# A recurrent attention with a gated projection: the list scheduler's order replaced by one written order

## Chip, cores and metric

The kernel runs on one core of one Trainium2 chip, in one launch. The metric is the device time of the launch in microseconds (us), median of several runs.

## The reference, cut to what matters

```
# r, k, v, w, a, b: (B=4, H=8, S=768, D=40); moe_w_a, moe_w_b: (320, 1536); moe_w_out: (1536, 320)
state = zeros(B, H, D, D)
for t in range(S):
    y[t]  = r[t] @ state                         # per batch and head
    Sa    = state @ a[t]
    state = state * w[t] - outer(Sa, b[t]) + outer(v[t], k[t])
x = y as (B*S, H*D)                              # 3072 x 320
out = ((x @ moe_w_a) * (x @ moe_w_b)) @ moe_w_out
```

The first half is a recurrence over 768 tokens for 32 pairs of batch and head. The second half is a gated projection of the 3072 rows that it gives.

## The kernel before

The 768 tokens are cut into 12 chunks of 64 (n = 0 to 11), and each chunk's 32 heads into two halves (c = 0, 1). Inside a chunk the recurrence is written as matrix products with the inverse of a triangular 64x64 matrix per head. The work is planned as 3159 operations, each a short run of instructions of one engine. They come from these functions inside `wkv_moe`:

- `prep(n, c)` loads a half chunk (`W`, `BK`, `A`), runs two scans and a reciprocal over it on VectorE (`Q<-W`, `d`, `pe<-W`), multiplies (`BK<-BK,Q`, `A<-A,pe`), computes 64 small products on TensorE (`scores`: `at<-A,BK`) and transposes (`nat`: `at<-ident,BK`), masks a part on VectorE (`TK<-at,tri`), copies the other on ScalarE (`AB<-at`) and stores all of it by DMA to `un_d`, from where `un` is loaded later.
- `lanes(g)` inverts the triangular matrices of a group of one or two chunks on VectorE, 15 or 31 steps of two instructions (`Yt<-Y,N` and `Y<-Y,Yt`), between one transposition at its start (`N<-AB`) and two at its end (`TC<-Y` and `T<-Y`). `T` is the list's name for the tile `T3`.
- `join(n)` and `merge(n)` put the inverses together on TensorE (operations `xt`, `t3`, `tc_`, `l2a`, `l2b`; tiles `T,AB`, `W,TC`, `TC,W`).
- `main(n, c)` is the recurrence itself: on TensorE `r_`, `u_`, `s_`, `g_`, `y_` and `sd_`, between them copies on ScalarE and products on VectorE. The state of a half is in `ST`; it is updated by a sum and a product (`ST<-at,ST`, `ST<-ST,pcs`), and `sd_` transposes it (`at<-ident,ST`). The output goes to `X` and by DMA to `x_d`.
- `pack(n)` loads a chunk's rows back and splits them into two parts of lower precision (`xk`).
- `plan_tile(f)` and `plan_lazy(f)` load one of 12 tiles of the three weights (`wraw`) and decode it, in some 13 operations each piece on VectorE, ScalarE and GpSimd (`w_ex`, `w_mt`, `w_rs`, then `wt` or `wo`).
- `unit(n, f)` is one chunk's rows times one tile of the weights: 16 matmuls into `ab`, the product of the two halves (`g`), its split into `gh` and `gl`, and six matmuls into `po` (operation `second`). There are 144 units. Five of the tiles are used while the recurrence runs, the seven others after it, for all chunks.

What sets the order: `Plan.op` notes each operation with its engine, an estimate of its duration, what it reads and writes, and a rank `v`. `Plan.run` (line 158 on) is a list scheduler. It keeps a clock for each engine, takes the engine that can start first, and on it, among the operations that can start within 0.05 us of the first, the one with the lowest rank. It also hands out the four PSUM banks `at` (`Banks`, `need`, `free`). The chosen operation is emitted at once, and every engine runs its instructions in the order of emission; SP issues all DMAs in that order too. So a waiting instruction holds everything behind it on its engine. `InOrder` keeps the framework from moving anything.

All instructions that pass through `InOrder` carry its line, 72 in the profile before (203 after). So the rows below are told apart by their tiles.

## Time and profile before

| what | us |
|---|---|
| median of 3 runs (their range) | 796.56 (795.31 to 804.69) |
| span of the profiled execution, first to last instruction | 799.3 |
| TensorE (PE) busy in it | 705.0 |
| VectorE (DVE) busy in it | 573.6 |
| ScalarE (ACT) busy in it | 417.0 |
| mean granted TensorE clock, share of 2.4 GHz | 0.889 |

The profiled execution lies 2.7 us above the median and within the range of the runs. What lies around its span is not told apart from it, so a sum made in its trace is carried to the median by that difference. A busy time is a sum over stages with different limits, and a stretch is therefore read by its own row.

### The profile page before, as it was taken

To read this page: it belongs to the slowest core of one execution; us is meant where nothing else is said; L and a number is where in the kernel's file an instruction comes from. 1 tells how busy PE (TensorE), PEld (TensorE's weight loads), DVE (VectorE), ACT (ScalarE), POOL (GpSimd) and SP (SyncE) were. 2 spreads that over 40 slices of the span, in tenths; PEclk is the share of its full clock that TensorE was granted. 3 is DMA by queue.
4 is the path that set the end of the run, shared out by engine and by line. 5 is a ranking of instruction groups with operands and counts; after the bars stand their busy time and mean duration, and the time that the engine had idled before them with its cause. 6 is when DMAs were issued, how large, how long until landed. Compare 5 with 4: busy or idle time off the path is not lost.

```text
span 799.3 us, 31281 instructions
## 1 busy us (share of the span) xinstructions
PE 705.0 (88%) x13509; PEld 665.0 (83%) x13509; DVE 573.6 (72%) x1161; ACT 417.0 (52%) x1080; POOL 195.9 (25%) x242
## 2 busy tenths in 40 slices
PE   5446757889789999899899999999999999999996
PEld 3346646878679998789888898999999999999996
DVE  8779798678978998898898684675676574233244
ACT  4438637636666577458555454855764443222221
POOL 6000203200120121102011010364546563222221
PEclk9555655789769999999999698999999999999999
DMA  6879886496878688977857367747621210000023
GB/s 195 245 212 275 257 246 196 114 276 205 234 231 262 194 221 242 292 248 199 260 161 210 88 219 214 212 118 195 197 75 54 58 42 5 1 1 2 1 78 125
DMA packets 99915, 133.05 MB, mean 166 GB/s; under 512 B 28554, under 2 KB 76026, under 8 KB 96954
## 3 DMA queue, kind: packets, MB, share of 16 engines
q1 hardware_dynamic: 99770, 130.97, 54.9%
q8 instruction: 108, 1.77, 0.9%
q14 instruction: 37, 0.30, 0.1%
HBM read 87.86 MB, written 38.43 MB: 158 GB/s over the span
## 4 chain that ended last, share of the span: by engine, by line
PE 75%; DMA 10%; issue 4%; DVE 4%; ACT 3%; SPq 2%; POOL 1%; ACTq 0%; DVEq 0%; POOLq 0%
PE ab L72 34%; PE at L72 26%; PE po L72 15%; DMA BK<-in_bk_dram 2%; DMA un_d<-bkn 2%; SPq L72 2%; DMA un<-un_d 1%; DMA wraw<-in_wa_dram 1%; DMA acc<-po_d 1%; DMA un_d<-TK 1%; DMA xf<-x_d 1%; DMA W<-in_wd_dram 1%; DMA SV<-in_vn_dram 1%; ACT T L72 1%; DMA A<-in_ai_dram 1%
## 5 line engine op out<-in xcount | busy, mean ns | idle before, releaser
L72 PE MATMUL ab<-xk,wt 120*128 120x256 f32 x2304 | 310.7, 289 | 2.0 <-issue 1.5
L72 PEld LDWEIGHTS ab<-xk,wt 120*128 120x128 f32 x2304 | 294.2, 195 | 5.1 <-issue 1.8
L72 POOL TENSOR_TENSOR gl<-g,gh 128x256 fp32r<-128x256 f32 x134 | 108.8, 813 | 367.2 <-ACT gh L72 338.7
L72 PE MATMUL po<-wo,gh 128*128 128x320 f32 x576 | 151.2, 316 | 3.7 <-ACT w_rs L72 2.8
L72 DVE TENSOR_TENSOR g<-ab,g 128x256 f32<-128x256 f32 x144 | 60.7, 422 | 112.4 <-ACT g L72 111.9
L72 ACT COPY g<-ab 128x256 f32<-128x256 f32 x144 | 53.7, 373 | 125.2 <-PE ab L72 120.7
L72 PEld LDWEIGHTS po<-wo,gh 128*128 128x128 f32 x576 | 102.1, 189 | 2.6 <-ACT gh L72 0.8
L72 ACT CAST gh<-g 128x256 fp32r<-128x256 f32 x144 | 58.4, 406 | 71.9 <-PE po L72 36.3
L72 PE MATMUL po<-wo,gl 128*128 128x320 f32 x288 | 89.2, 310 | 0.0
L72 DVE TENSOR_TENSOR Y<-Y,Yt 128x31 f32<-128x31 f32 (+20 forms) x185 | 64.2, 347 | 6.4
L72 PE MATMUL at<-SV,un 128*64 128x40 f32 (+1 forms) x1472 | 53.3, 238 | 16.8 <-DMA SV<-in_vn_dram 11.0
L72 PEld LDWEIGHTS at<-SV,un 128*64 128x64 f32 (+1 forms) x1472 | 47.7, 149 | 22.7 <-issue 16.5
L72 DVE TENSOR_TENSOR Yt<-Y,N 128x31 f32<-128x31 f32 (+20 forms) x185 | 63.6, 344 | 3.9
L72 DVE TENSOR_TENSOR acc<-po,acc 128x320 f32<-128x320 f32 x96 | 43.8, 487 | 24.7 <-PE po L72 24.7
L72 PEld LDWEIGHTS po<-wo,gl 128*128 128x128 f32 x288 | 54.8, 190 | 2.9 <-DVE Y L72 2.9
L72 PE MATMUL at<-A,BK 64*64 64x64 f32 x1536 | 36.4, 256 | 17.6 <-DVE A L72 10.3
L72 PEld LDWEIGHTS at<-A,BK 64*64 64x64 f32 x1536 | 32.4, 166 | 21.6 <-issue 12.4
L72 POOL TENSOR_TENSOR w_mt<-w_mt,wt 120x384 f32<-120x384 f32 x22 | 23.8, 1083 | 87.6 <-ACT wt L72 74.4
L72 ACT COPY AB<-at 32x256 f32<-32x256 f32 (+1 forms) x72 | 31.5, 437 | 22.4 <-PE at L72 19.5
L72 ACT COPY SV<-at 64x160 f32<-64x160 f32 x96 | 27.4, 286 | 21.9 <-PE at L72 20.6
L72 DVE TENSOR_TENSOR G<-at,tri 128x512 f32<-128x512 f32 x48 | 30.9, 683 | 11.2 <-PE at L72 10.8
L72 PE MATMUL at<-T,AB 32*32 32x32 f32 x1152 | 23.2, 213 | 16.9 <-DVE T L72 7.7
(108 smaller groups left out, 1155.2 us busy)
## 6 DMA issues: line engine op xcount, KB each, us to landing
un<-un_d SPq DMA_DIRECT2D x22, 1092.0 KB
BK<-in_bk_dram SPq DMA_DIRECT2D x22, 448.0 KB
rv<-in_rvf_dram SPq DMA_DIRECT2D x22, 448.0 KB
un_d<-bkn SPq DMA_DIRECT2D x22, 320.0 KB
x_d<-X SPq DMA_DIRECT2D x24, 256.0 KB
un_d<-pe SPq DMA_DIRECT2D x22, 260.0 KB
un_d<-A SPq DMA_DIRECT2D x44, 128.0 KB
un_d<-TK SPq DMA_DIRECT2D x44, 128.0 KB
```

What stands on the lines that cost most here:

```text
L72: r = fn(*args, **kwargs)
```

## The change

`Plan.run` no longer chooses. It takes a list of the 3159 operations' numbers and emits them in that order. The clock of each engine is still kept, because the banks are still chosen by it. The branch for filler work, which was not in use, and two switches that were always on are gone. Two dependencies that held before because of the old order are stated: the second copy into `SV` (operation `uc`) reads what the first wrote, and the second product into `X` reads what the first wrote. Both pairs run on one engine each, ScalarE and VectorE. No operation is added or removed, and each has the same instructions as before; the tiles `at` that it gets may differ.

```
+ORDER = """
+0 3 4 8 5 2 7 1 6 15 19 21 24 22 27 25 26 16 17 18 23 28 243 20 43 246 247 266 9 11 13 244 12 32 248 33 29 40 62 34 38
...
+"""
...
-    def run(self, slack=0.05, switch=0.13):
+    def run(self, order, switch=0.13):
...
-        while todo:
...
-                s0 = min(s for s, _ in c)
-                s, o = min(((s, o) for s, o in c if s <= s0 + slack), key=lambda x: (x[1].v, x[1].seq))
...
+        assert sorted(order) == list(range(len(self.ops)))
...
+        for k in order:
+            o = self.ops[k]
+            assert o.left == 0
+            s = max(engines[o.eng], o.ready)
...
-            pl.op("ACT", 2 * act(160), uc, [("u", q)], [(*kS, j)] if j == 0 else [kS])
+            pl.op("ACT", 2 * act(160), uc, [("u", q), (*kS, 0)] if j else [("u", q)], [kS] if j else [(*kS, 0)])
...
-                in1=PEt[:, gq * 4:gq * 4 + 4, 0:C]), [("y", q), kU], [(*kX, gq)] if gq == 0 else [kX], free=[(ps, gq)], v=v + 0.15)
+                in1=PEt[:, gq * 4:gq * 4 + 4, 0:C]), [("y", q), kU, (*kX, 0)] if gq else [("y", q), kU], [kX] if gq else [(*kX, 0)], free=[(ps, gq)], v=v + 0.15)
...
-    pl.run()
+    pl.run([int(k) for k in ORDER.split()])
```

Where the order changes, at three places. First VectorE, at the beginning of the first inverse (`lanes` of chunk 0; `BK_182`, `A_184` are chunk 1's first half, `BK_183` its second). Before:

```order
L72 TENSOR_TENSOR BK_182<-BK_182,Q_180 128x1024
L72 STREAM_TRANSPOSE N<-AB 128x32x32
L72 TENSOR_TENSOR A_184<-A_184,pe_188 128x512
L72 TENSOR_TENSOR BK_183<-BK_183,Q_181 128x1024
L72 TENSOR_TENSOR AB<-AB,off 128x16x32
L72 SCALAR_TENSOR_TENSOR Q_180<-W_178,one 128x521
L72 TENSOR_TENSOR TK_186<-at_65,tri 128x512
L72 RECIPROCAL d_190<-Q_180 128x8
L72 SCALAR_TENSOR_TENSOR pe_188<-W_178,d_190 128x520
L72 TENSOR_TENSOR Yt<-Y,N 128x30
```

The same place now:

```order
L203 STREAM_TRANSPOSE N<-AB 128x32x32
L203 TENSOR_TENSOR AB<-AB,off 128x16x32
L203 TENSOR_TENSOR Yt<-Y,N 128x30
L203 TENSOR_TENSOR Y<-Y,Yt 128x2x15
L203 TENSOR_TENSOR Yt<-Y,N 128x56
L203 TENSOR_TENSOR Y<-Y,Yt 128x2x2x14
L203 TENSOR_TENSOR BK_182<-BK_182,Q_180 128x1024
L203 TENSOR_SCALAR w_ex_163<-wraw_161 120x384
L203 TENSOR_TENSOR Yt<-Y,N 128x78
L203 TENSOR_TENSOR Y<-Y,Yt 128x2x3x13
L203 TENSOR_SCALAR w_mt_164<-wraw_161 120x384
```

The inverse starts ahead of chunk 1's loaded products, the product `BK_183` is 24 places later, and the first steps of the weight decode stand among the inverse's steps.

Second, VectorE at the end of the same inverse (here `BK_182`, `A_184` are chunk 2's first half). Before:

```order
L72 TENSOR_TENSOR Y<-Y,Yt 128x2x15
L72 STREAM_TRANSPOSE TC<-Y 128x32x32
L72 TENSOR_TENSOR A_184<-A_184,pe_188 128x512
L72 STREAM_TRANSPOSE T_197<-Y 128x32x32
L72 TENSOR_TENSOR BK_183<-BK_183,Q_181 128x1024
L72 TENSOR_TENSOR TK_186<-at_66,tri 128x512
L72 TENSOR_TENSOR A_185<-A_185,pe_189 128x512
```

Now:

```order
L203 TENSOR_TENSOR Y<-Y,Yt 128x2x15
L203 TENSOR_TENSOR w_mt_164<-w_mt_164,wt_232 120x384
L203 STREAM_TRANSPOSE T_197<-Y 128x32x32
L203 SCALAR_TENSOR_TENSOR Q_181<-W_179,one 128x521
L203 RECIPROCAL d_190<-Q_181 128x8
L203 TENSOR_TENSOR TK_187<-at_66,tri 128x512
L203 SCALAR_TENSOR_TENSOR w_ex_163<-wraw_162,w_ex_163 120x384
L203 TENSOR_TENSOR A_184<-A_184,pe_188 128x512
L203 TENSOR_TENSOR BK_182<-BK_182,Q_180 128x1024
```

`T` now comes ahead of `TC` (which follows six rows further on), and chunk 2's products `A_184` and `BK_182` come behind `T`, where they were ahead of it.

Third, VectorE at chunk 2's second half: the state's sum and product (`ST_212`) and the steps of the inverse of chunks 3 and 4. Before:

```order
L72 TENSOR_TENSOR Y<-Y,Yt 128x20x12
L72 TENSOR_TENSOR ST_212<-at_66,ST_212 128x8x40
L72 TENSOR_TENSOR ST_212<-ST_212,pcs 128x8x40
L72 TENSOR_TENSOR Yt<-Y,N 128x231
L72 TENSOR_TENSOR Y<-Y,Yt 128x21x11
L72 TENSOR_TENSOR G<-at_63,tri 128x512
L72 TENSOR_TENSOR G<-at_65,tri 128x512
```

Now (the sum `ST_212<-at_63,ST_212` stands three rows ahead of these):

```order
L203 TENSOR_TENSOR X_215<-at_64,un_200 128x256
L203 TENSOR_TENSOR X_215<-at_66,un_200 128x256
L203 TENSOR_TENSOR Yt<-Y,N 128x112
L203 TENSOR_TENSOR Y<-Y,Yt 128x28x4
L203 TENSOR_TENSOR Yt<-Y,N 128x87
L203 TENSOR_TENSOR Y<-Y,Yt 128x29x3
L203 TENSOR_TENSOR Yt<-Y,N 128x60
L203 TENSOR_TENSOR Y<-Y,Yt 128x30x2
L203 TENSOR_TENSOR Yt<-Y,N 128x31
L203 TENSOR_TENSOR Y<-Y,Yt 128x31
L203 TENSOR_TENSOR TK_186<-at_64,tri 128x512
L203 TENSOR_TENSOR ST_212<-ST_212,pcs 128x8x40
```

The state's product is no longer behind its sum but behind the inverse's last steps.

## Rows read from the trace of the kernel before

**Rows 1.** The page: busy time by engine, and the chain that ended last.

```profile
PE 705.0 (88%) x13509; PEld 665.0 (83%) x13509; DVE 573.6 (72%) x1161; ACT 417.0 (52%) x1080; POOL 195.9 (25%) x242
...
PE 75%; DMA 10%; issue 4%; DVE 4%; ACT 3%; SPq 2%; POOL 1%; ACTq 0%; DVEq 0%; POOLq 0%
```

**Rows 2.** Busy time by stretch: window, length, engines' busy us (instructions), clock, DMA share, GB/s.

```profile
0.00:90.00 90.00, 49.89 (x1316) 41.62 (x1317) 76.17 (x125) 48.91 (x125) 17.18 (x36) 0.66 0.77 232
90.00:118.00 28.00, 15.73 (x413) 13.50 (x411) 23.50 (x52) 11.22 (x30) 2.83 (x4) 0.56 0.87 259
118.00:150.00 32.00, 25.15 (x843) 23.05 (x844) 25.55 (x42) 23.78 (x58) 8.01 (x7) 0.50 0.63 178
150.00:209.00 59.00, 49.94 (x1423) 45.75 (x1424) 47.17 (x113) 31.78 (x85) 5.60 (x7) 0.93 0.74 218
209.00:240.00 31.00, 25.96 (x728) 23.94 (x721) 25.25 (x41) 20.35 (x55) 7.97 (x8) 0.62 0.81 229
240.00:560.00 320.00, 306.19 (x6988) 286.03 (x6988) 257.04 (x538) 187.99 (x502) 60.64 (x70) 0.96 0.70 208
560.00:780.00 220.00, 219.55 (x1732) 219.29 (x1731) 111.13 (x239) 89.43 (x221) 90.04 (x108) 1.00 0.16 47
```

**Rows 3.** Waits of DVE from 0 to 118 us: total us, times, longest us.

```profile
DVE BK L72 <- DMA BK<-in_bk_dram: 6.7, 3, 4.4
DVE G L72 <- PE at L72: 2.7, 1, 2.7
...
DVE Q L72 <- DMA W<-in_wd_dram: 1.1, 2, 0.6
DVE A L72 <- DMA A<-in_ai_dram: 0.9, 1, 0.9
```

**Rows 4.** Timeline of DVE, 20 to 56 us: start, us, form [idle before <- releaser].

```profile
24.75 1.22 DVE L72 TENSOR_TENSOR BK<-BK,Q 128x1024 f32<-128x1024 f32 x1 [1.82 <-DMA BK<-in_bk_dram]
...
42.70 1.23 DVE L72 TENSOR_TENSOR BK<-BK,Q 128x1024 f32<-128x1024 f32 x1 [4.38 <-DMA BK<-in_bk_dram]
...
50.29 2.00 DVE L72 STREAM_TRANSPOSE T<-Y 128x1024 f32<-128x1024 f32 x1
```

**Rows 5.** Timeline of PE at the two inverses' ends, 44 to 64 and 105 to 122 us.

```profile
50.51 1.99 PE L72 MATMUL at<-A,BK 64*64 64x64 f32 x64 [8.01 <-DVE A L72]
...
113.70 1.93 PE L72 MATMUL at<-T,AB 32*32 32x32 f32 x128 [4.37 <-DVE T L72]
117.96 1.00 PE L72 MATMUL at<-A,BK 64*64 64x64 f32 x25 [2.33 <-DVE A L72]
120.28 1.34 PE L72 MATMUL at<-A,BK 64*64 64x64 f32 x39 [1.32 <-issue]
```

**Rows 6.** Waits of PE from 114 to 240 us, and over the whole span.

```profile
PE at L72 <- issue: 10.7, 10, 2.8
PE at L72 <- DVE T L72: 3.3, 1, 3.3
PE po L72 <- ACT w_rs L72: 2.8, 1, 2.8
...
PE at L72 <- issue: 24.5, 23, 2.8
```

**Rows 7.** Timeline of PE, 196 to 222 us: one operation at either clock, a transposed state, an inverse waited for.

```profile
199.37 0.58 PE L72 MATMUL at<-ident,ST 104*128 104x104 f32 x4
...
200.84 1.16 PE L72 MATMUL at<-A,BK 64*64 64x64 f32 x64
...
208.26 1.20 PE L72 MATMUL at<-T,AB 32*32 32x32 f32 x64 [3.33 <-DVE T L72]
...
215.10 1.99 PE L72 MATMUL at<-A,BK 64*64 64x64 f32 x64
```

**Rows 8.** Timeline of DVE around 191 us: the state's sum and product.

```profile
191.26 0.48 DVE L72 TENSOR_TENSOR ST<-at,ST 128x320 f32<-128x320 f32 x1
191.78 0.49 DVE L72 TENSOR_TENSOR ST<-ST,pcs 128x320 f32<-128x320 f32 x1
```

More of the change, by code (lines that the diff above doesn't have):

```diff
@@ L169, in run @@
         clock = Clock()
-        ready = {e: [] for e in engines}
         for o in self.ops:
@@ L174, in run @@
                 d.users.append(o)
[L175 to L177 removed]
+        assert sorted(order) == list(range(len(self.ops)))
         log = []
[L179 to L205 removed]
+        for k in order:
+            o = self.ops[k]
+            assert o.left == 0
+            s = max(engines[o.eng], o.ready)
+            if o.port:
+                s = max(s, port["DVE" if o.eng == "POOL" else "POOL"])
             if o.need:
[L207 to L209 removed]
+                o.need.ids, s = self.banks(o.need.n, s)
+                for b in o.need.ids:
+                    self.bank_free[b] = None
             d = o.dur
@@ L214, in run @@
                 last_mode = o.mode
-                if CLK:
-                    t = engines["PE"]
-                    if self.filler and s - t > 0.4:
-                        share = FILL if clock.full(t) else FILLC
-                        nf = int(share * (s - t) / (0.09 if clock.full(t) else 0.17))
-                        for _ in range(nf):
-                            self.filler()
-                            t = clock.run(t, 0.09, 384)
-                        self.nfill = getattr(self, "nfill", 0) + nf
-                        s = max(s, t)
-                    d = clock.run(s, d, o.work) - s
-                if FETCH and o.pairs:
+                d = clock.run(s, d, o.work) - s
+                if o.pairs:
                     pairs += o.pairs
@@ L244, in run @@
                 o.end = max(s + d, ring) + 1.8 + DMARGIN
-            for bk, k in o.free:
-                self.bank_free[bk.ids[k]] = o.end
+            for bk, b in o.free:
+                self.bank_free[bk.ids[b]] = o.end
             o.fn()
-            todo -= 1
             log.append((s, o))
@@ L252, in run @@
                 u.ready = max(u.ready, s + d if u.eng == o.eng and not o.moved else o.end)
-                if not u.left:
-                    ready[u.eng].append(u)
         self.log, self.busy = log, busy
```

30 lines of the change are left out of this document (removed), and 126 rows, old and new, of the table ORDER.

## The prediction

> **What bounds the kernel now.** I read four views in this order: the page with its chain that ended last, the busy time by stretch, the waits of VectorE and TensorE, and the timelines around the places where the order changes.
>
> The page says that TensorE is busy for 705.0 us and that 75% of the chain lies on it; DMA is 10%, pauses that nothing in the profile explains ("issue") 4%, VectorE 4% [rows 1]. The mean hides two programs in one. From 560 to 780 us TensorE is busy for 219.55 of 220 us at full clock, and from 240 to 560 for 306.19 of 320 [rows 2]. The last 220 us cannot gain anything from an order, and the 320 before them at most 13.8 us. The rest must come from the first 240 us, where TensorE works for 49.89 + 15.73 + 25.15 + 49.94 + 25.96 = 166.7 us and is idle for 73.3.
>
> In the first 118 us the engine that comes nearest to its bound is VectorE: 76.17 + 23.50 = 99.7 us busy [rows 2]. TensorE waits for it there: 8.01 us for the product `A` ahead of chunk 2's `scores`, 4.37 us for the inverse `T`, 2.33 us for `A` again [rows 5]. So ahead of 118 us the time is VectorE's work plus VectorE's own waits. These waits are 6.7 us for `BK`, 2.7 us for TensorE (`G`), 1.1 us for `W` and 0.9 us for `A`, together 11.4 us, of which the three loads are 8.7 [rows 3]. The remaining 18.3 - 11.4 = 6.9 us are the start and small gaps.
>
> The clock is the second limit. It is granted at 0.50, the lower level, through all of 118 to 150 us, at 0.62 from 209 to 240, and at 0.93 to 1.00 elsewhere behind 150 [rows 2]. The same 64 `scores` matmuls take 1.16 us at the upper level and 1.99 at the lower [rows 7], so an operation loses 42% of its time when the clock rises.
>
> **The change part by part.** Nothing is added or removed, so the sum is made of waits that go or come. The sum of the work on each engine stays.
>
> *The two stated waits.* Each is between two instructions of one engine, which runs them in that order anyway. Cost 0; nothing can stand behind them longer than before.
>
> *VectorE in the first inverse.* Ahead of the first `T` now go: two scans and a reciprocal (2.7 us together), one product `BK` (1.22 us, [rows 4]), one `A` (0.69), one mask (0.68) and the transposition `TC` (2.0, as `T` in [rows 4]): 7.3 us leave. Seven decode steps of 0.36 to 0.56 us enter: 3.3 us. `T` is thus 4 us of work earlier. But TensorE does not profit as it stands: in its order, which hardly moves, chunk 2's `scores` stand ahead of the operation `xt` that needs this `T`, and they need chunk 2's `A_184` and `BK_182`, which now come behind `T` on VectorE (second place of the change). Counting VectorE's work ahead of that gate with the durations of the trace, it is 38.9 us before and 41.4 now. Before, TensorE started there at 50.51 [rows 5], so 11.6 us of idling and starting lay ahead. If all of that stays, the gate is 2.5 us later; if the two long waits for `BK`, 1.82 and 4.38 us [rows 4], are covered by the decode and the inverse's steps that now stand ahead of these products, it is 2.5 - 6.2 = -3.7 us.
>
> *VectorE up to 118 us.* The same count up to the `scores` at 117.96 [rows 5] gives 99.2 us of work before and 99.5 now. Whatever the front gains is therefore idle time of VectorE and nothing else. What changes in its favour: products that wait for a load stand 12 to 25 places later in VectorE's row, with steps that need no load ahead of them (first place of the change). Against it: the load has to come too. The DMA engines are 0.77 and 0.87 busy in these stretches [rows 2], so a load is often late because the queue is full, and a wait moved to a later product may meet the next load instead. Bounds: all 11.4 us of [rows 3] go and 3.5 of the small gaps, -14.9; or no wait goes, the 2.5 us of the first gate stay, and a load whose issue on SP is held by a transposition costs 1.5 more, +4. I take -6, somewhat more than half of the waits named in [rows 3], near what the first gate's two rows give (-6.2).
>
> *150 to 240 us.* TensorE waits here once for an inverse, 3.33 us at 208.26 [rows 7], the same wait that [rows 6] have. VectorE's work ahead of that `T` (chunks 3 and 4) is 2.1 us more than before; ahead of the next three groups it is 2.7, 2.2 and 0.4 us less. On the other side six of the state's products move 6 to 12.5 us later in VectorE's work (third place of the change). The transposition `sd_` on TensorE needs them. The product ended at 191.78 + 0.49 = 192.27 [rows 8] and `sd_` started at 199.37 [rows 7], so 7.1 us of delay are covered there, and behind it stand 3.3 us that would have been idle anyway. I take -1, with +5 (12.5 - 7.1 = 5.4, of which the 3.3 us of idling may absorb part, at one or two places) and -9 (the 3.3 us of `T` and as much again of other waits, and the three groups' 5.3 us partly) as ends.
>
> *Issue pauses.* TensorE has 24.5 us in 23 pauses that no event explains, the longest 2.8 us, 10.7 of them between 114 and 240 us [rows 6]; one is the 1.32 us at 120.28 that cuts 64 `scores` into 25 and 39 [rows 5]. A wait of 2.8 us labelled `w_rs` [rows 6] has the same length. Counted along TensorE's instruction stream they stand 128 or 256 matmuls apart, or a multiple of it, and not at one kind of operation. TensorE has as many instructions as before, so I expect as many pauses, at other operations: 0, with 6 us either way, a quarter of 24.5, since a pause may now fall into a wait, or out of one. The Trainium skill, in "Runtime: NRT & Kernel Launch", section "Instruction fetch mechanics", has crossing an instruction block cost a tail that is mostly hidden; the 2.8 us pauses of this trace are not hidden, and by that page's rule the term would be 0 with nothing either way.
>
> *The clock.* Where waits go, the clock may rise sooner. Between 118 and 150 us TensorE spends 25.15 us at the lower level; at the upper it would be 42% less, 10.5 us. Between 209 and 240 some 20 of the 25.96 us are at the lower level (a mean of 0.62 lies three quarters of the way down from 1.0 to 0.5), worth 8.4 us. Together -19 at best; +10 if a stretch that is now at the upper level falls. TensorE's own order in both stretches stays nearly as it was, so I take only -3, for a rise that comes some us sooner.
>
> *The last 560 us.* 240 to 560 has 13.8 us of idling, and the new order cannot fill most of it, since pauses remain; TensorE's 219.55 of 220 us behind that is work. 0.
>
> **Sum:** 0 - 6 - 1 + 0 - 3 + 0 = -10 us. The profiled execution spans 799.3 us, so its like would be 789.3; the median of the runs is 2.7 us lower, 796.56, and the forecast there is 786.5.
>
> **Rivals.**
>
> *The clock rises in both slow stretches.* If the waits of 4.37, 2.33 and 3.33 us [rows 5, 7] go, TensorE works without a break where it now stops, and the lower level may end at 118 instead of 150 and not return at 209. Price: 6 + 10.5 + 8.4 = 25 us, 771.5. For it: between 150 and 209 us the level is 0.93 with 49.94 us of 59 busy, and between 209 and 240 it is 0.62 with nearly the same share, 25.96 of 31 [rows 2]; so the two levels stand close to each other, and a small thing decides. Against it: the operations and their order in these stretches stay. The Trainium skill, in "TensorE: Matmul & The Clock Gate", section "HAM oscillation — how this bites in real kernels", has the clock fall back when TensorE waits between bursts, and so speaks for this rival; the nearly equal busy shares at 0.93 and 0.62 say that waits alone don't decide here. By that rule the time would be 771.5.
>
> *The waits only change place.* The loads set the pace: DMA is 0.77 and 0.87 busy to 118 us [rows 2], and 8.7 of VectorE's 11.4 us of named waits are loads [rows 3]. What VectorE no longer waits for at one product it waits for at the next, the clock stays, and the time is 796.5. Against it: the long waits are single ones, 1.82 and 4.38 us [rows 4], and not a rate.
>
> *The state's products come too late, slower.* Six of them stand 6 to 12.5 us later on VectorE, some behind an inverse's last steps. Where `sd_` on TensorE waits for one of them, the next chunk's `r_` and all units behind it wait. The cover is 7.1 us at the one place shown [rows 7, 8]; from there on each us of delay is a us of the kernel. With the 3 us by which a delay of 10 us passes that cover, and nothing of it absorbed, six such places cost 18 us, less the 6 of the front: 12, so about 808. It decides where a product's delay exceeds 7 us while TensorE has no other work in its row. Against it: only two of the six move by more than 7.1 us in this count, and TensorE has units between most halves.
>
> **How the numbers follow.** The forecast has 0.50 with a range of its own of 779 to 795; the clock's rise 0.25, at 771.5; waits that change place 0.15, at 796.5; the late states 0.10, at 808. About 2% is what a measurement of this kernel can tell from no change: below 780.6 or above 812.5 us. Faster by more than that: nearly all of the clock's case, 0.23, and 0.10 from the lower part of the forecast, together 0.33. Slower by more: 0.07, of the late states and a little of the waits. Within 2%: 0.60. The range: 770 keeps the greater half of the clock's case and leaves out about a tenth; 803 leaves out most of the late states' case, the other tenth.
>
> **What would show it.** Right: VectorE's waits for `BK` up to 118 us fall from 6.7 us to 1 or 2, the `scores` of [rows 5] start at 45 to 48 instead of 50.51 and at about 112 instead of 117.96, and the mark at which TensorE becomes full, near 240, moves by about 10 us; from there to the end the two traces have the same length. Wrong, by the first rival: a granted clock over 0.8 between 118 and 150 or 209 and 240. By the second: VectorE's idle time to the second gate is still 18 us, under other names. By the third: TensorE's waits for `ST` at `sd_`, of 3 us or more, at several chunks. If the pauses sum to less than 18 us or more than 31, that term was wrong.

## The result and the profile after

The changed kernel takes 807.12 us (median of 20 runs, 800.15 to 822.05); the kernel before takes 797.51 in runs on the same chip (20 runs, 788.04 to 807.56). The ratio is 1.0131, with a 95% interval of 1.0104 to 1.0159: slower, by about 10 us. That is less than 2%, but the interval lies clear of 1. The forecast was 786.5 with a range of 770 to 803, so it is wrong in sign and the range does not hold the result. Ratios here and below are formed from the fast runs of either kernel alone and medians from all runs, so the two can differ.

The page of the changed kernel, with the lines that answer to [rows 1] and its instruction queue:

```profile
PE 697.1 (87%) x13509; PEld 656.8 (82%) x13509; DVE 576.0 (72%) x1161; ACT 410.6 (51%) x1080; POOL 194.8 (24%) x242
...
q1 hardware_dynamic: 99770, 130.97, 56.2%
q8 instruction: 108, 1.77, 0.9%
...
PE 74%; DVE 8%; DMA 7%; issue 6%; ACT 2%; SPq 1%; POOL 1%; DVEq 0%; ACTq 0%; POOLq 0%
```

On the chain of waits DMA went from 10% to 7%, "issue" from 4% to 6% and VectorE from 4% to 8%. The stretches of [rows 2], in the changed kernel:

```profile
0.00:90.00 90.00, 47.67 (x1279) 39.03 (x1281) 78.86 (x136) 47.38 (x121) 17.77 (x36) 0.64 0.75 217
90.00:118.00 28.00, 18.21 (x619) 15.69 (x619) 26.30 (x50) 17.60 (x46) 5.08 (x7) 0.74 0.85 248
118.00:150.00 32.00, 23.92 (x710) 21.42 (x700) 23.82 (x42) 19.57 (x48) 9.55 (x7) 0.53 0.75 221
...
209.00:240.00 31.00, 24.21 (x695) 22.24 (x696) 20.50 (x35) 16.56 (x44) 4.64 (x6) 0.61 0.73 199
240.00:560.00 320.00, 299.96 (x6978) 280.67 (x6977) 257.61 (x534) 187.48 (x508) 55.87 (x70) 0.98 0.73 213
```

VectorE is busy for 78.86 + 26.30 = 105.2 us of the first 118 where it was for 99.7. So it got denser, as forecast. Its waits in that stretch, to be held against [rows 3] (total us, times, longest):

```profile
DVE A L203 <- DMA A<-in_ai_dram: 3.7, 1, 3.7
DVE BK L203 <- DMA BK<-in_bk_dram: 2.3, 2, 1.8
```

`BK` fell from 6.7 to 2.3 us, `A` rose from 0.9 to 3.7. TensorE's timeline at the two gates of [rows 5] (start, us, form, idle before):

```profile
46.37 1.99 PE L203 MATMUL at<-A,BK 64*64 64x64 f32 x64 [1.35 <-DVE BK L203]
...
105.65 1.93 PE L203 MATMUL at<-T,AB 32*32 32x32 f32 x128
112.37 2.05 PE L203 MATMUL at<-A,BK 64*64 64x64 f32 x64
```

The first `scores` start at 46.37 instead of 50.51 and the others at 112.37 instead of 117.96: 4.1 and 5.6 us earlier. The gain of the front is there. It does not arrive: counted in TensorE's work, the two profiled executions are level again between 165 and 240 us. The view that shows what took its place is that of TensorE's waits. From 0 to 250 us, first before, then after:

```profile
PE at L72 <- issue: 13.7, 13, 2.8
...
PE at L72 <- DVE T L72: 7.7, 2, 4.4
```

```profile
PE at L203 <- issue: 23.8, 16, 2.7
PE at L203 <- DVE BK L203: 14.6, 3, 6.8
...
PE at L203 <- issue: 15.0, 13, 3.6
PE ab L203 <- issue: 3.2, 2, 2.5
...
PE at L203 <- DVE ST L203: 0.3, 1, 0.3
```

The last three rows are of 250 to 570 us. The waits for `T` (7.7 us) are gone from the front's rows, and the pauses that no event explains rose from 13.7 to 23.8 us there and, behind 250, from 10.8 + 1.5 to 15.0 + 3.2 + 0.2.

The label "issue" is not the same as a late instruction. The section on what a pause is, below, ties these pauses to packets of instructions, each of which brings a block of 127 or 128 matmuls with their weight loads. By that two rows stand on the wrong side. Before:

```profile
171.05 0.31 PE L72 MATMUL po<-wo,gh 128*128 128x320 f32 x1 [2.83 <-ACT w_rs L72]
...
211.39 1.93 PE L72 MATMUL at<-SV,un 128*64 128x40 f32 x32 [1.93 <-DMA un<-un_d]
```

The first cuts one `second` in two, and its matmul does not read `w_rs`; it stands where such a block ends, 1.4 us behind the landing of the next one's packet, so it is a pause, as the prediction suspected of this wait. And the changed kernel's 2.24 us at 210.41, the last row shown under "What held" below, is labelled "issue" but starts no block and follows the last packet by 8.7 us: it ends 0.09 us after the last of the 16 landings of the load of `un`, so it is the same wait as the 1.93 us before. The tables below count both as what they are.

One profile is one execution, and a kernel's executions lie up to 15 us from their median. So two executions of either order are set beside each other, each pair chosen for nearly the same busy time of TensorE (that is, the same share of the lower clock). "Pauses" is the sum of TensorE's waits labelled "issue" over the whole span, "waits" that of all its other rows, with the two rows above moved.

| | span | busy | pauses | waits | rest |
|---|---|---|---|---|---|
| old order, written down (e2) | 793.7 | 697.5 | 25.7 | 63.6 | 6.9 |
| changed kernel | 801.6 | 697.1 | 39.9 | 57.1 | 7.5 |
| before | 799.3 | 705.0 | 28.8 | 59.2 | 6.3 |
| changed kernel again (e1) | 809.8 | 705.4 | 38.7 | 58.3 | 7.4 |

The first pair differs by 7.9 us: busy -0.4, pauses +14.2, waits -6.5, rest +0.6. The second differs by 10.5: busy +0.4, pauses +9.9, waits -0.9, rest +1.1. The mean, 9.2, is close to the medians' 9.6. The change takes 3.7 us of waits away on the mean, and brings 12.1 us of pauses.

### The profile page after: what moved, and what is told of

It reads as the page before. It is cut to its first block, busy times and chain, and to the rows that moved or that the text cites. A ratio compares the mean times of both kernels' runs of the same rounds, so it can differ in the third digit from the quotient of the medians.

```text
span 801.6 us, 31230 instructions
## 1 busy us (share of the span) xinstructions
PE 697.1 (87%) x13509; PEld 656.8 (82%) x13509; DVE 576.0 (72%) x1161; ACT 410.6 (51%) x1080; POOL 194.8 (24%) x242
## 3 DMA queue, kind: packets, MB, share of 16 engines
q1 hardware_dynamic: 99770, 130.97, 56.2%
q8 instruction: 108, 1.77, 0.9%
## 4 chain that ended last, share of the span: by engine, by line
PE 74%; DVE 8%; DMA 7%; issue 6%; ACT 2%; SPq 1%; POOL 1%; DVEq 0%; ACTq 0%; POOLq 0%
PE ab L203 34%; PE at L203 25%; PE po L203 15%; DMA BK<-in_bk_dram 3%; DVE Yt L203 1%; DVE Y L203 1%; DMA un<-un_d 1%; DMA un_d<-bkn 1%; SPq L203 1%; DVE pe L203 1%; DMA rv<-in_rvf_dram 1%; DVE G L203 1%; DVE BK L203 1%; DMA A<-in_ai_dram 1%; DMA un_d<-TK 1%
## 5 line engine op out<-in xcount | busy, mean ns | idle before, releaser
L203 PE MATMUL ab<-xk,wt 120*128 120x256 f32 x2304 | 305.2, 287 | 3.2 <-issue 3.2
L203 PEld LDWEIGHTS ab<-xk,wt 120*128 120x128 f32 x2304 | 289.4, 193 | 6.4 <-issue 3.7
L203 POOL TENSOR_TENSOR gl<-g,gh 128x256 fp32r<-128x256 f32 x134 | 104.8, 786 | 379.8 <-ACT gh L203 340.7
L203 PE MATMUL po<-wo,gh 128*128 128x320 f32 x576 | 145.1, 313 | 1.4 <-DVE acc L203 1.1
L203 ACT COPY g<-ab 128x256 f32<-128x256 f32 x144 | 53.1, 373 | 117.4 <-PE ab L203 109.4
L203 ACT CAST gh<-g 128x256 fp32r<-128x256 f32 x144 | 57.7, 406 | 87.1 <-PE po L203 53.1
L203 PEld LDWEIGHTS po<-wo,gl 128*128 128x128 f32 x288 | 54.4, 189 | 0.0
L203 PE MATMUL at<-A,BK 64*64 64x64 f32 x1536 | 34.7, 248 | 22.1 <-DVE A L203 12.3
L203 PEld LDWEIGHTS at<-A,BK 64*64 64x64 f32 x1536 | 30.7, 159 | 25.8 <-issue 18.9
L203 PE MATMUL at<-ident,BK 104*128 104x104 f32 x192 | 29.5, 301 | 19.2 <-DVE BK L203 13.3
L203 POOL TENSOR_TENSOR w_mt<-w_mt,wt 120x384 f32<-120x384 f32 x22 | 25.9, 1177 | 78.2 <-ACT wt L203 71.8
L203 ACT COPY AB<-at 32x256 f32<-32x256 f32 (+1 forms) x72 | 31.4, 437 | 25.8 <-PE at L203 24.5
L203 PEld LDWEIGHTS at<-ident,BK 104*128 104x128 f32 x192 | 22.7, 166 | 22.4 <-issue 14.3
```

The costliest lines, as they stand in the source:

```text
L203: r = fn(*args, **kwargs)
```

## The experiments

After e2 two theories were left. **Pauses:** TensorE stops because its instructions come late, and the new order makes that more frequent. **Fit:** the new order is simply worse matched, engine to engine. The rivals within the first were that the pauses hang on where instruction blocks happen to be cut (so that any shift would do), or on how much data traffic there is. This table holds the two sums of every run, from TensorE's wait views, ahead of and behind 250 us. As above, a row labelled "issue" that starts no block of instructions is counted with the waits. In e3, e5, e13, e16, e17 and e18 that is the same wait for `un`, with 2.0 to 3.2 us. In e6, e7, e9, e10, e11, e14 and e17 it is others in the first 85 us, the most in e11 (12.4 us), e10 (6.1) and e14 (5.6), and e11 has one of 2.1 us behind 250. Each experiment was run beside the kernel before on its own chip, whose median is given with it.

| run | pauses to 250 | waits to 250 | pauses 250-570 | waits 250-570 |
|---|---|---|---|---|
| before | 16.5 | 56.4 | 12.3 | 2.0 |
| e2 old order written | 13.1 | 62.0 | 12.7 | 0.8 |
| e4 old, new from 250 | 8.7 | 63.8 | 19.0 | 1.6 |
| e8 old, units bunched | 14.4 | 59.2 | 16.0 | 8.0 |
| e15 old, pauses thinned | 10.5 | 61.0 | 8.9 | 8.5 |
| changed | 21.6 | 54.4 | 18.4 | 1.6 |
| e1 changed again | 20.1 | 56.4 | 18.7 | 0.8 |
| e3 new, old from 250 | 15.9 | 54.5 | 8.5 | 3.0 |
| e5 new, units spread late | 16.9 | 55.8 | 3.5 | 19.9 |
| e6 new, units spread | 17.2 | 58.0 | 6.1 | 16.2 |
| e7 new, 64 matmuls more | 26.6 | 47.2 | 16.4 | 1.3 |
| e13 new, thinned late | 16.4 | 54.5 | 8.1 | 5.4 |
| e14 new, thinned | 15.9 | 57.9 | 8.7 | 6.7 |
| e16 new, thinned, all engines | 19.9 | 62.4 | 10.1 | 3.4 |
| e17 new, more traffic | 20.3 | 58.4 | 21.3 | 5.7 |
| e18 new, less traffic | 21.7 | 53.1 | 12.6 | 2.9 |
| e9 new, old DMA order | 13.7 | 79.4 | 14.4 | 12.6 |
| e11 old, new DMA order | 17.4 | 77.6 | 13.1 | 17.4 |
| e10 new, old elementwise | 16.7 | 100.4 | 9.5 | 41.3 |
| e12 old, new elementwise | 11.3 | 87.9 | 4.7 | 60.2 |

### e1 and e2: the same again, and the old order written down

e1 is the changed kernel without an edit. e2 is the changed kernel with the list scheduler's own sequence as its list, so it has the new code and the stated waits but the old order.

```
-ORDER = """0 3 4 8 5 2 7 1 6 15 19 21 24 22 27 25 ...
+ORDER = the sequence in which before.run() emitted the operations
```

> The changed kernel itself, again, for a second profile of it. All theories: slower than before by about 1.3% (807 against 797.5). Theory P (pauses): TensorE's issue pauses, 24.5 us in 23 before and 38.7 us in 29 in the changed kernel's first profile, are again near 39 or more, since the new order puts the stretches with many short matmuls at times when the DMA queues are full. Theory D (VectorE): the pauses are chance and come out anywhere from 20 to 40; what is stable are TensorE's waits for VectorE, 26.9 us for BK and A in the changed kernel's first profile against 17.0 before.

> The changed kernel with the list scheduler's own order written into it as the list. Instructions and their order on each engine are those of before, only two of the four PSUM banks change names at some places. All theories: no change, ratio 0.997 to 1.003; a second profile of the order of before. Theory P: issue pauses near 25 us again. Theory D: they may be anywhere from 20 to 40. Rival N (the way in which the order is given costs something by itself, for instance by other bank names): about 1.013.

e1: 800.91 against 792.84, ratio 1.0122 [1.0062, 1.0183]. e2: 793.66, ratio 1.0027 [0.9981, 1.0074]. The medians lie 8.1 and 0.8 us over before. The loss is repeated, and it belongs to the order alone; the two stated waits cost nothing that can be measured, as forecast.

### e3 and e4: one half of the order each

```
+ORDER = NEW[:952] + [k for k in OLD if k not in NEW[:952]]
```

is e3 (new until about 250 us), and e4 is the other way about:

```
+ORDER = OLD[:940] + [k for k in NEW if k not in OLD[:940]]
```

> The new order up to the operations planned for about 250 us, then what is left in the old order. Theory D (loss in the front, where VectorE is near its bound): as slow as the changed kernel, about 807. Theory P with pauses all over: about half the loss, 802. Theory L (the loss arises behind 250 us, where TensorE is saturated and each pause is lost): 797.

> The old order up to the operations planned for about 250 us, then what is left in the new order. Theory D: as before, 797. Theory P: about 802. Theory L: about 807.

e3: 798.9, ratio 1.0155 [1.0091, 1.0218]. e4: 799.78, ratio 1.0152 [1.009, 1.0213]. Either half costs about as much as the whole, by the ratios and by the medians (6.1 and 6.9 us beside e1's 8.1), so the losses do not add, and none of the three theories has that. In the sums e4 has the old front (8.7 and 63.8) and the new rear (19.0); e3 has the new front (15.9 and 54.5) and the old rear (8.5). So the pauses go with the order of their own half. e3's profiled execution was the fastest of its six (787.4, the others 798.0 to 808.3), and its sums would make it faster than before; why its median is not stays open.

### e5 and e6: fewer dense runs, by moving units

A dense run is a stretch in which TensorE passes 128 matmuls in 4 us or less, between the units' long ones. e5 moves 51 single operations on TensorE, most of them units and their `second`, into such runs behind 250 us; e6 moves four more ahead of 250. Two of the places in e5, by the operations' numbers in the list:

```
-1823:second 2064:r_ 2052:g_ 2066:u_ 1845:half 1846:half 1838:half 1839:half 1830:second
+2064:r_ 1832:half 1823:second 2052:g_ 1845:half 1846:half 1838:half 1839:half 2066:u_ 1830:second
...
-1454:y_ 1472:s_ 1319:half 1320:half
+1319:half 1320:half 1454:y_ 1472:s_
```

> The changed kernel, with 51 of TensorE's 432 unit operations behind 250 us moved by one to six places on TensorE, into the stretches with many short matmuls, so that each run of 128 matmuls lasts longer than the wait for its successor; the orders on VectorE, ScalarE, GpSimd and SP stay. Theory P (the loss lies in TensorE's issue pauses, which come where 128 short matmuls follow each other): pauses behind 250 us fall from 18.3 and 18.7 us to 6 or less, nothing takes their place, and the time is 8 to 12 us under that of the changed kernel: a ratio to before of 0.997 to 1.004. Theory D (VectorE's and the loads' order): no change, 1.013. Rival W (the moved units wait for ScalarE and VectorE instead): pauses fall, TensorE's other waits rise by as much, 1.010.

> As the run before it, with units moved in the first 250 us too (55 moved in all). Theory P: the pauses of 23.7 and 20.1 us up to 250 us also fall, by 4 to 8 us; together 12 to 18 us under the changed kernel, a ratio of 0.990 to 0.998, so faster than before. Theory D: 1.013. Rival W: 1.005 to 1.013, with more waits of TensorE for ScalarE and VectorE.

e5: 817.38 against 796.02, ratio 1.0289 [1.0234, 1.0344]. e6: 817.18, ratio 1.0291 [1.0235, 1.0348]. A miss: the pauses behind 250 fell as they should, to 3.5 us, but the waits there rose to 19.9, as e5's wait view of TensorE from 250 to 570 us shows:

```profile
PE at L204 <- ACT W L204: 4.4, 3, 2.5
PE ab L204 <- DVE g L204: 4.3, 5, 1.4
PE at L204 <- issue: 3.5, 5, 1.5
PE at L204 <- ACT uT L204: 3.2, 3, 1.9
```

Against the changed kernel that is -15 of pauses and +18 of waits. TensorE's busy time is larger too, 709.1 us against 697.1 and 705.4 in the two profiles of the changed kernel, which these sums leave out. A unit put ahead of a step of the recurrence holds that step, and what other engines wait for in turn. Pauses can be taken out, then, but not at any price.

### e7: the same order, shifted by 64 matmuls

```
+for j in range(32):
+    mul(AT[j % 4][0:32, 0:1], ident[0:32, 0:32], T_[0].rearrange("p m t -> p (m t)")[0:32, 0:1])
 for t in AT:
     mul(t, ident, ...)
```

> The changed kernel with 32 tiny matmuls more (64 in the trace) ahead of TensorE's first work, where it is idle; the order is untouched. Theory P: the pauses stand where they do because of the count of instructions, so all of them move to other operations, by 64 matmuls; their sum changes by up to 10 us either way (between 28 and 50) and the time with it. Theory D: the pauses' places and the time stay (1.013), or pauses move and their sum stays near 40.

e7: 807.8 against 796.02, ratio 1.015 [1.0085, 1.0216]. The trace has 13573 matmuls instead of 13509, half an instruction block more, ahead of all others. Pauses of 16.4 instead of 18.4 us behind 250 and 43.0 instead of 39.9 in all: they stand at other operations now, and sum to nearly the same. With this one other cut, then, the loss is no accident of where blocks end.

### e8: the old order made denser

```
-1366:nat 1368:nat 1109:l2b 1206:l2a 855:second
+855:second 1366:nat 1368:nat 1109:l2b 1206:l2a
...
-1195:half 1196:half 1451:g_
+1451:g_ 1195:half 1196:half
```

Twenty units are moved in this way, in the old order, out of runs that are then dense.

> The old order with 20 of TensorE's unit operations behind 250 us moved by one to four places, away from the stretches with many short matmuls; all other engines keep the old order. Theory P: pauses behind 250 us rise from 12.3 and 12.7 us to some 20, a ratio to before of 1.007 to 1.012, nearly the loss of the changed kernel by TensorE's order alone. Theory D: 1.000.

e8: 812.97, ratio 1.0254 [1.0187, 1.0321]. Pauses behind 250 rose from about 12.5 to 16.0 us, waits from 1 or 2 to 8.0. The direction is the expected one, but the waits take the larger part, so this run shows less than it was meant to.

### e9 to e12: one engine group's order alone

In e9 the new order keeps everything but its row of DMAs on SP, which comes from the old one but for the few that have to stand elsewhere (387 of 443 DMAs change place); e11 is the old order with the new row. e10 and e12 do the same with the rows of VectorE, ScalarE and GpSimd. A piece of SP's row, new and old:

```
-14 263 290 267 268 311 400 253 252 379
+277 400 268 267 290 252 253 263 291 311
```

> The changed kernel with SP's order (all DMAs) put back to that of before, by TensorE's progress; TensorE, VectorE, ScalarE and GpSimd keep the new order. Theory S (the new order of the DMAs makes TensorE's instruction blocks wait longer behind data: 2.4 us of delay per block from 120 to 250 us against 1.7, 1.4 against 1.05 behind 400): pauses fall from about 41 to 30 us or less and the ratio to before to 0.995 to 1.003. Theory T (TensorE's own order makes them) and theory E (the order of VectorE, ScalarE and GpSimd): still 1.010 to 1.015. Theory M (the orders fit each other, and any mixture loses): 1.015 or more, with new waits of VectorE for loads.

> The changed kernel with the orders of VectorE, ScalarE and GpSimd put back to those of before; TensorE and SP keep the new order. Theory S: still slow, 1.012 to 1.02, since the gain of 6 us of waits in the first 120 us goes too. Theory T: the same as S here. Theory E: 0.998 to 1.004. Theory M: 1.015 or more.

> The kernel before with the new order of the DMAs alone. Theory S: pauses rise from 26 to 36 us or more, a ratio of 1.008 to 1.015. Theories T and E: 0.997 to 1.003, pauses near 26. Theory M: 1.01 or more, with new waits of VectorE for loads, the pauses as before.

> The kernel before with the new orders of VectorE, ScalarE and GpSimd alone; TensorE and SP keep the old order. Theories S and T: 0.990 to 0.998, since the front's gain of 6 us comes without the pauses. Theory E: 1.008 to 1.015. Theory M: 1.01 or more.

Against 798.53: e9 840.55, ratio 1.0529 [1.0451, 1.0607]; e10 943.32, 1.1807 [1.1721, 1.1893]; e11 847.6, 1.0609 [1.053, 1.0687]; e12 971.13, 1.2196 [1.2096, 1.2296]. None of these mixtures is near either kernel: 5 to 22% of loss, most of it in waits. The two orders fit in themselves, and no part of the loss can be found by swapping one engine group's row. TensorE's waits to 250 us, e9 first (new order, old DMA row), then e11:

```profile
PE at L204 <- DVE A L204: 25.9, 2, 13.3
PE at L204 <- DVE BK L204: 17.5, 3, 6.5
PE at L204 <- issue: 13.6, 9, 3.1
```

```profile
PE at L204 <- issue: 29.8, 15, 8.2
PE at L204 <- DMA un<-un_d: 10.5, 2, 10.0
```

The 29.8 us mislead: the two longest, 8.17 us at 55.65 and 4.19 at 81.54, start no block and stand 7.0 and 2.6 us behind the last packet. What is left is 17.4 us; in e9, with its one pause of 2.7 us under `ab` and without one of 2.6 us that comes ahead of any packet, it is 13.7. In the table the seven runs with the old DMA row have 8.7 to 16.5 us of pauses ahead of 250, 12.6 on the mean, and the thirteen with the new one 15.9 to 26.6, 19.0 on the mean, whatever the other engines do. That points to the transfers, but the two ranges touch, and each run is one profile.

### What a pause is

TensorE's instructions come over the queue named "instruction" on the page: 108 packets, 1.77 MB, 16.4 KB each, one for every 127 or 128 matmuls with their weight loads. Of the rows labelled "issue", all 24 before and 31 of 32 after end 1.2 to 1.7 us after such a packet has landed; the last one is the wait for `un`. By the packets' times a packet is asked for about when TensorE enters the block ahead of it, and not whole blocks earlier: in some 160 of the 174 blocks of both traces up to 540 us it starts 0 to 5 us after that moment, and it takes 0.88 to 2.7 us. Four blocks of the changed kernel, and three of before, worked out from the packets' and the matmuls' times in the trace (us):

| block entered at | passed in | packet starts after | takes | pause |
|---|---|---|---|---|
| 395.5, after | 3.53 | 2.56 | 0.88 | 1.51 |
| 440.7, after | 2.86 | 3.16 | 0.95 | 2.53 |
| 476.2, after | 3.44 | 3.28 | 1.27 | 2.68 |
| 510.8, after | 2.38 | 3.26 | 1.29 | 3.57 |
| 393.9, before | 7.06 | 3.11 | 0.88 | none |
| 422.0, before | 4.86 | 4.22 | 0.96 | 1.62 |
| 491.6, before | 8.77 | 3.05 | 1.18 | none |

Start plus duration plus 1.4 us less the time in which the block is passed gives the pause: 3.26 + 1.29 + 1.4 - 2.38 = 3.57, and in the others of the table to within 0.2 us (the 1.4 is about the middle of the 1.2 to 1.7, so this is a reckoning and no separate proof). A packet that starts 3 us late shows nothing where the block holds a unit and lasts 7 us, and stops TensorE where the block is a dense run of small matmuls. The last of the four in TensorE's timeline, and what the DMA engines did around it (508 to 521 us in 40 slices of 0.325 us, busy tenths; queues; transfers issued):

```profile
516.72 0.26 PE L203 MATMUL at<-RH,T 64*64 64x40 f32 x3 [3.57 <-issue]
...
DMA  9998999999999979879567998998557310000000
...
q8 instruction: 2, 0.03, 1.3%
...
rv<-in_rvf_dram SPq DMA_DIRECT2D x1, 448.0 KB
wraw<-in_wb_dram SPq DMA_DIRECT2D x1, 360.0 KB
```

The DMA engines are full when the packet is asked for, with the 448 KB of `rv` issued at 508.44 among other transfers; the 360 KB of `wraw` are issued at 514.06, as the packet starts. On average a packet starts 2.42 us after its block's predecessor is entered in the changed kernel's blocks of 100 to 250 us (1.79 before), and 1.70 us behind 250 (1.44 before).

It is not that the new order has more dense blocks. Behind 250, 21, 20 and 21 blocks are passed in less than 4.5 us with the new order there (changed, e1, e4), and 19, 19 and 20 with the old one (before, e2, e3). What differs is how late the packet starts that is asked for in them: 1.83, 1.84 and 1.58 us after the block is entered, on the mean, against 1.14, 0.95 and 1.16. For all other blocks it is 1.24 to 1.44 against 1.32 to 1.47. So the new order's late packets fall to the blocks that cannot hide them.

The Trainium skill, in "Runtime: NRT & Kernel Launch", section "Instruction fetch mechanics", has the instruction store refilled in blocks of 16 KiB by a queue of its own while the engine runs, and the packets here agree. It calls the crossing mostly hidden; by these traces that holds for 83 of the 108 blocks before and 77 after, and the others sum to 28.8 and 39.9 us.

### e13 to e16: thin the pauses, with a price on waits

Here the moves were chosen by both numbers: the pause that each block would have, and the wait that a move would cause, both worked out from the traces. e13 moves 35 operations on TensorE in the new order behind 250 us, e14 61 in the whole of it, e15 35 in the old order behind 250, e16 101 on all engines in the new order.

```
-1823:second 2064:r_ 2052:g_ 2066:u_ 1845:half 1846:half 1838:half 1839:half 1830:second
+2064:r_ 1832:half 1823:second 2052:g_ 1845:half 1846:half 1838:half 1839:half 2066:u_ 1830:second
...
-1507:half 1759:l2b
+1759:l2b 1507:half
```

are two places of e13. e14 adds such as these ahead of 250:

```
-412:scores 234:t3
+234:t3 412:scores
...
-451:l2a 739:nat
+739:nat 451:l2a
```

and one place of e15, in the old order, is

```
-1506:half 1759:l2b 1856:l2a
+1759:l2b 1856:l2a 1506:half
```

> The changed kernel, with 35 of TensorE's unit and recurrence operations behind 250 us moved by one to six places (where a moved operation needs it, the copy it waits for on ScalarE moves along), chosen by two conditions from the traces: a run of 128 matmuls that meets a late instruction block gets a unit, and no operation is moved ahead of what it waits for. Theory P (pauses are the loss): pauses behind 250 us fall from 16 to 19 us to about 8, TensorE's other waits there stay under 4 us (the run with 51 units moved had 20), and the time is 5 to 9 us under the changed kernel's: ratio to before 1.002 to 1.008. Theory W (whatever the pauses give, waits take): other waits rise as much, 1.012 or more.

> The same with 61 operations from the whole recurrence, the first 250 us too. Theory P: pauses in all fall from 39 to 43 us to about 22 to 28, other waits stay near 54 us, 10 to 16 us under the changed kernel: 0.992 to 1.000. Theory W: pauses fall, other waits rise by as much, 1.01 or more.

> The old order with 35 operations behind 250 us moved by the same conditions. Theory P: pauses behind 250 us fall from 12.3 and 12.7 us to about 5, other waits there stay under 4 us, 4 to 7 us under before: 0.991 to 0.996. Theory W: 1.000 or more.

> The changed kernel with 101 single moves on all engines, chosen by the same conditions and by TensorE's and VectorE's waits. Theory P: as the run with 61 moves or 2 us better, 0.990 to 0.999. Theory W: 1.01 or more.

Against 793.0: e13 797.76, ratio 1.0066 [1.0037, 1.0096]; e14 798.82, 1.0034 [0.9991, 1.0076]; e15 795.92, 1.0037 [1.0006, 1.0068]; e16 803.67, 1.016 [1.0104, 1.0216]. e13's wait view of TensorE from 250 to 570 us:

```profile
PE at L204 <- issue: 6.4, 5, 2.3
PE ab L204 <- issue: 1.7, 2, 1.0
PE at L204 <- DVE G L204: 1.5, 1, 1.5
```

With 5 + 2 pauses instead of 16 the rear has 8.1 us of them, ten less than the changed kernel, and 3.8 more of waits: -6.5 by the sums, and 1.0131 - 1.0066 = 0.65% or 5 us by the ratios. This is the direct test: the same kernel with fewer pauses behind 250 gives back half of the loss by the ratios, and 3.3 of e1's 8.1 us by the medians on that chip. The blocks there that are passed in under 4 us went from 14 to 6. e14 gives back three quarters by its ratio, with an interval that touches 1, but by its median it is no nearer to before than e13 (5.8 us over it, e13 4.8), and its sums ahead of 250 are hardly better than the changed kernel's. e15 is the counter-test, and a miss, since 4 to 7 us of gain were expected: in the old order there were only 12 us to thin, 3.4 of them went, 6.5 of waits came, and it is 0.4% slower than before. e16 was a miss: moves on the other engines brought the waits to 250 up to 62.4 and the gain was gone. None of the complete kernels tried beats the one before.

### e17 and e18: the traffic, up and down

```
+if n >= 5:
+    nc.sync.dma_start(out=dram.tile([P, rvf.shape[-1]], F32, name=f"more{n}_{c}"), in_=rvf[n, c])
```

in `main`, beside the store of `x_d`, gives e17 fourteen transfers more behind 250 us; the order of all else stays. e18 cuts fourteen loads to one of their rows, 4 KB, instead, so that these chunks work on older rows and the output is not that of the reference:

```
-load(lambda: (RV.rearrange("p x m t -> p (x m t)"), rvf[n, c]), ...
+RVs = RV.rearrange("p x m t -> p (x m t)")
+load(lambda: (RVs, rvf[n, c]) if n < 5 else (RVs[0:1], rvf[n, c][0:1]), ...
```

> The changed kernel with 14 copies of 512 KB more, from DRAM to a DRAM place that nothing reads, one behind each X store of the chunks from 5 on (behind 250 us). Theory Q (an instruction block of TensorE is late because it queues behind data on the same DMA engines): the delay from a block's request to its first byte rises behind 250 us from 1.4 to 1.9 us to 2 us or more, pauses there from 16 to 19 us to 25 or more, and the time by 5 to 15 us, to 1.02 to 1.03 of before. Theory R (a block's delay has nothing to do with data traffic; the pauses follow from TensorE's count of short matmuls alone): pauses there stay at 16 to 19 us, 1.010 to 1.015, unless TensorE waits for late loads.

> The changed kernel with the loads of r and v (448 KB each, 14 of them) of the chunks from 5 on cut to 4 KB, so that these chunks work on older rows; all instructions and their order stay. Theory Q: the blocks' delay falls and with it the pauses behind 250 us, from 16 to 19 us to 12 or less, the time by 4 to 8 us, to 1.002 to 1.008 of before. Theory R: pauses there stay at 16 to 19 us and the time at 1.010 to 1.015.

e17: 825.41 against 797.42, ratio 1.0304 [1.0219, 1.0389]. e18: 800.2, ratio 0.9954 [0.9908, 1.0000]; its twelve runs lie between 788.3 and 810.9, so that the medians and the ratio disagree on the side of before on which it lies. Beside the changed kernel it is faster by either: 2.8 us over the median of before instead of 9.6, or 1.0131 - 0.9954 = 1.8%. The data queue on the page, e17 first, and TensorE's pauses from 250 to 570 us:

```profile
q1 hardware_dynamic: 100218, 138.31, 57.7%
...
PE at L203 <- issue: 18.9, 12, 4.6
...
PE ab L203 <- issue: 1.5, 2, 1.2
PE po L203 <- issue: 0.9, 1, 0.9
```

```profile
q1 hardware_dynamic: 98006, 124.61, 53.6%
...
PE at L203 <- issue: 8.0, 11, 1.6
PE ab L203 <- issue: 4.6, 2, 3.4
```

With 138.31, 130.97 and 124.61 MB the pauses behind 250 are 21.3, 18.4 and 12.6 us, and a packet's mean delay there is 1.78, 1.70 and 1.43 us. The instructions of TensorE are the same in all three. The profiles with the new order behind 250 and the same traffic (changed, e1, e4, e7) have 16.4 to 19.0 us. So e18, by its one profile, lies clearly below them: with less data moving the pauses fall. e17 lies above them, but by less than they differ among themselves, and under the 25 us and the delay of 2 us that were expected, so the rise is in the right direction and no more. They are not all of e17's loss: 3 of about 14 us, beside 4 more of waits and 9 more of busy time at the lower clock in its profiled execution.

## Why the prediction was wrong

**What held.** VectorE's work does stand ahead of TensorE's to 118 us, and the gain is idle time of VectorE: -6 was forecast to the second gate, -5.6 came. The stated waits cost nothing. (Of the 6.9 us that it calls start and small gaps, 3.6 were named waits too; only the lower bound of its term uses some of them.) The 3.33 us for `T` at 208.26 [rows 7] became 0.45:

```profile
195.66 0.48 DVE L203 TENSOR_TENSOR ST<-at,ST 128x320 f32<-128x320 f32 x1
200.89 0.48 DVE L203 TENSOR_TENSOR ST<-ST,pcs 128x320 f32<-128x320 f32 x1
...
201.95 0.52 PE L203 MATMUL at<-ident,ST 104*128 104x104 f32 x4
...
205.83 1.20 PE L203 MATMUL at<-T,AB 32*32 32x32 f32 x64 [0.45 <-ACT bkn L203]
...
210.41 1.94 PE L203 MATMUL at<-SV,un 128*64 128x40 f32 x32 [2.24 <-issue]
```

The state's product does stand 5.2 us behind its sum now, and `sd_` starts 0.6 us after it. But TensorE waits nowhere for 3 us at `ST`; the only such row behind 250 is 0.3 us. So the late-state rival was wrong, and that its 808 lies next to the measured 807.12 is chance. Over the runs that have one of the two orders unchanged on all engines to 250 us, the waits there are 60.5 us on average in the old order (before, e2, e4, e8, e15) and 55.3 in the new (changed, e1, e3, e5, e13, e17, e18): -5.2, where the two terms of the sum had -7.

**The step that failed** is the term "issue pauses", put at "0, with 6 us either way", with the words that TensorE "has as many instructions as before, so I expect as many pauses, at other operations". It measured +14.2 and +9.9 us in the two pairs, and with 39.9 and 38.7 us the changed kernel is over the 31 us that the prediction named as the sign that this term was wrong. (The 24.5 us that it started from are one row; with 1.5 us at `ab` and the 2.8 us labelled `w_rs` before had 28.8.) The reading ahead of it was right (pauses stand 128 or 256 matmuls apart, or a multiple) and the conclusion was not: with 108 blocks and 25 pauses, most blocks show none, so the number of blocks fixes nothing. What decides is how late a block's packet starts and how quickly the block ahead of it is passed, and the order sets both: from one list to the other at least 227 of TensorE's 678 operations have to be moved, 180 of them behind 250 us, and 206 of the 443 DMAs. To 250 us the mean of the same runs is 12.6 us of pauses in the old order and 19.0 in the new. With the waits that is 73.1 and 74.3: the whole gain of the front is eaten there. Behind 250, where the prediction had 0 "since pauses remain", they went from 11.2 us (before, e2, e3) to 18.7 (changed, e1, e4), and the waits only from 1.9 to 1.3. The last row above is no such pause but the wait for `un`, 2.24 us where it was 1.93: the 3.33 us saved at 205.83 are not lost there but in pauses around it, such as those of 2.67 us at 182.29 and 2.53 at 229.80.

**The clock**, put at -3, did not move where it was looked for: 0.53 for 0.50 from 118 to 150 us, 0.61 for 0.62 from 209 to 240. The pairs cannot show what it costs over the whole span, since they were chosen for equal busy time. The mean granted clock of all runs on one chip is 0.893 against before's 0.898 for e1, and 0.893 against 0.893 for e7, so no clear difference. The first rival, the clock's rise, was wrong.

**The second rival** was right in that the front's gain does not arrive, and wrong in the place and the size: it had VectorE going on to wait for loads. VectorE did get rid of most of that. It is TensorE that goes on to wait for its own instructions, and with the front's gain gone, what is lost behind 250 is the result. The sum as it came out: -4 of waits, +12 of pauses, +1 of small gaps (means of the two pairs), and nothing of the clock that can be told.

Shown by runs: that the order alone makes the loss (e1, e2); that the pauses fall with less traffic (e18) and keep their sum when blocks are cut elsewhere (e7); that fewer of them give time back (e13). Only argued: that the new DMA row is what makes packets late at the dense blocks; e9 and e11 agree ahead of 250 (13.7 and 17.4 us), but with so much else changed that they don't prove it. The theory of fit is not excluded beside the pauses: e5, e8 and e9 to e12 lose mostly by waits, and e13 gives back only half. Open: e3's median, and why each half costs as much as both. A wider search for an order with few pauses and few waits was not tried beyond e14 and e16.

## What to carry to other kernels

TensorE's instructions come here by transfers that no line of the kernel names, and with less data moving its pauses for them were shorter (e18): where a dense run of short instructions stands beside large loads, look for pauses that no event explains, hold each against the landings of the instruction queue before it is called one, and price them by packet delay plus duration against the time the block lasts, not by the number of blocks. An order that is tuned on waits alone does not see them. A long operation put into a dense run can hide a late packet, if it holds up nothing else (e13, not e5). And in this kernel moving one engine group's row in an order that was fitted as a whole cost far more than it could gain: 35 small moves with waits counted gave 0.65%, one row swapped cost 5 to 22%.

## What was not expected of the hardware

Several pauses come with a stretch at the lower clock. In the changed kernel, the stretch ahead of the pause that ends at 446.13, the pause's own operation, and what comes behind it; then the one behind the pause that ends at 516.72:

```profile
437.00:445.00 8.00, 6.60 (x270) 5.91 (x269) 7.31 (x21) 5.48 (x14) 0.61 (x1) 1.00 0.86 267
...
446.13 1.01 PE L203 MATMUL ab<-xk,wt 120*128 120x256 f32 x4 [2.53 <-issue]
...
445.20:452.00 6.80, 5.87 (x76) 5.36 (x75) 3.79 (x9) 2.47 (x6) 0.73 (x1) 0.50 0.08 21
...
516.90:520.30 3.40, 3.40 (x28) 3.24 (x22) 0.43 (x1) 2.91 (x9) 0.73 (x1) 0.50 0.28 75
```

The level goes from 1.00 (2.4 GHz) to 0.50 (1.2 GHz) with a pause of 2.53 us, although TensorE was busy for 6.60 of 8 us ahead of it and is so for 5.87 of 6.8 behind it. Before has it too, behind pauses of 1.56, 1.50 and 1.51 us. This is the longest, with the pause that ends at 444.91:

```profile
444.91 0.26 PE L72 MATMUL at<-T,RH 64*40 64x64 f32 x3 [1.50 <-issue]
...
445.10:458.70 13.60, 13.60 (x321) 12.72 (x318) 8.82 (x20) 5.62 (x14) 0.73 (x1) 0.50 0.11 32
```

Such a pause can cost more than its own length, if it is what brings the level down; no run tests that. It did not show as a difference between the orders: from 250 to 570 us the level is at 0.50 for 23.9 and 27.3 us in the two profiles of the old order (before, e2), and for 13.7 and 27.3 in those of the new one (changed, e1).
